# Float32 attention and two gated layers on one core: 36 subtractions of low halves go from GpSimd to VectorE

## The chip, the cores and the metric

The kernel runs on one core of one Trainium2 chip. The metric is device time in microseconds (us), the median of several executions; lower is better. Five engines work side by side, each through its own queue in order: TensorE (PE: matmuls, and PEld: weight loads), VectorE (DVE), ScalarE (ACT), GpSimd (POOL) and SyncE (SP, which here issues DMAs). An engine waits at the head of its queue for semaphores that other engines or DMAs raise.

## The reference, cut to what matters

```python
scores = scale * q @ k.T                       # 4 batches, 8 heads, 576 positions, 64 columns
scores = where(mask, scores, -1e9)             # heads 0-3: the last 32; heads 4-7: every 4th of the last 128
attn = softmax(scores) @ v                     # -> x: 2304 tokens x 512
xn = x / sqrt(mean(x * x) + 1e-6) * rms_g
g = xn @ w_gate                                # 512 -> 1536
h = (silu(g) * (xn @ w_val)) @ w_out           # 1536 -> 512
g2 = h @ w_in2                                 # 512 -> 2048
out = (maximum(g2, 0) + alpha * minimum(g2, 0)) @ w_out2
```

## The kernel before, in words

Every large product is made of float16 halves. A float32 matrix is scaled and rounded to a high half (float16), and the low half is what the rounding left out. A product then takes three matmuls: high by high, high by low and low by high. So each operand needs two element-wise steps: ScalarE writes the high half, and another engine subtracts it from the float32 value to get the low half.

**Weights.** They arrive as 64-bit floats, 128 x 512 to a block: 36 blocks for the first layer (for each c of 0 to 11 one of w_gate, w_val and w_out) and 32 for the second. `load_w` (L188) issues the DMA on SP, `decode_w` (L197) makes float32 of a block by three VectorE instructions (L202, L203, L204). A scale must be known before a block is split: for w_gate and w_val it comes from a Gram product on TensorE over a chunk of blocks (`gram_w1`, L257; c of 0 to 2 first, then 3 to 11), whose maxima go through L255, `over_partitions` (L309, a small matmul, L312) and `root_scale`. `split_w` (L377) then makes the halves. ScalarE writes the high half (L381). For two blocks of three of the first layer VectorE makes the low half in one instruction that also scales (L386). For the third, ScalarE first writes the scaled block back (L383) and GpSimd subtracts (L384). In the second layer every second block goes to GpSimd.

**Tokens.** There are seven token blocks j: 0 and 1 have 256 tokens (the first 128 positions of two batches each), 2 to 5 have 384, and 6 has 256. A stage A of a block is the first layer, a stage B the second. Stage A takes c from 0 to 11: `mm1` (L857) makes 24 matmuls into PSUM, ScalarE takes a tanh (L872), VectorE makes the product t by L873 and L874, and ScalarE writes its high half (L876). `lo` (L879) makes the low half on GpSimd (L882). `mm2` (L891) then adds both halves times w_out to the sum acc, 6 matmuls of 512 columns in blocks 0 and 1. In block 0 the `mm2` come 12 values of c late, in block 1 they follow one c behind (LAG0 and LAG).

**Attention.** Its steps (groups of queries) are interleaved with the blocks before the block that needs them. Of interest here are the normalisation of the rows (L689 on ScalarE, L690 on VectorE, a power on GpSimd, L691, and the scaled row on VectorE, L692), the transposes of those rows on TensorE (L704), and the exponentials on ScalarE (L548).

**Order.** The program is recorded in the order that `slots` and `steps` give, but the framework's scheduler then sets the order of the instructions on each engine by priority and its own estimate of times. So an edit of one function also moves others.

Of the kernel before, what the change touches and what calls it, by code (L numbers as in the profile page):

```python
# [13 lines left out]
ALU = mybir.AluOpType  # L14
# [15 lines left out]
def kernel(  # L30
# [14 lines left out]
    nc = tc.nc  # L45
# [6 lines left out]
    NW1 = 3 * C1  # L52
# [60 lines left out]
    def band(m, rows, cols, c0, lo, hi, off=0):  # L113

        view = m[0:rows, c0:c0 + cols]
        nc.gpsimd.affine_select(
            out=view, in_=view, compare_op=ALU.is_ge, fill=NEG,
            base=off - lo, pattern=[[1, cols]], channel_multiplier=-1,
        )
        nc.gpsimd.affine_select(  # L120
            out=view, in_=view, compare_op=ALU.is_ge, fill=NEG,
            base=hi - off, pattern=[[-1, cols]], channel_multiplier=1,
        )
# [43 lines left out]
    def give(*slots):  # L167
        clock_[0] += 1
        for i in slots:
            free[i] = True  # L170
            given_back[i] = clock_[0]

    def one_slot():

        i = min((i for i in range(NSLOT) if free[i]), key=lambda i: (given_back[i], i))
        free[i] = False
        return i
# [30 lines left out]
    def dec(b):  # L208
        d = dec_at[b]
        return wb[:, d * 512:(d + 1) * 512]  # L210
# [5 lines left out]
    def half(b, l):  # L216
        d = hl_at[b]
        return wb16[:, d * 1024 + l * 512:d * 1024 + (l + 1) * 512]
# [11 lines left out]
    def chunk(c):  # L230
        return max(i for i in range(NCH) if ch0[i] <= c)
# [3 lines left out]
    def scale_of(b):  # L235
        if b >= NW1:
            return S_IN + (b - NW1) % 2
        ch = chunk(b // 3)
        return 2 * NCH + ch if b % 3 == 2 else 2 * ch + b % 3
# [132 lines left out]
        nc.vector.tensor_scalar(nal, al, -1.0, None, ALU.mult)  # L372

    n_split = [0]
    LO1, LO2 = 3, 2

    def split_w(b):  # L377
        s = scale_of(b)
        n_split[0] += 1
        hl_at[b] = one_slot()  # L380
        nc.scalar.activation(half(b, 0), dec(b), ACTF.Copy, scale=wsg[:, s:s + 1])  # L381
        if n_split[0] % (LO1 if b < NW1 else LO2) == 0:
            nc.scalar.activation(dec(b), dec(b), ACTF.Copy, scale=wsg[:, s:s + 1])  # L383
            nc.gpsimd.tensor_tensor(half(b, 1), dec(b), half(b, 0), ALU.subtract)  # L384
        else:
            nc.vector.scalar_tensor_tensor(half(b, 1), dec(b), wsg[:, s:s + 1], half(b, 0), ALU.mult, ALU.subtract)  # L386
        give(dec_at.pop(b))
# [466 lines left out]
    def ncols(j):  # L854
        return blocks[j][1]

    def mm1(j, c):  # L857
        T = ncols(j)
        xt = xy[j % NXY]
        if T <= 256:  # L860
            both = psw()
            pg, pv = both[:, 0:256], both[:, 256:512]
        else:
            pg, pv = psw(), psw()
        for ps, b in ((pg, b_g(c)), (pv, b_v(c))):
            n = 0
            for kc in range(KD):
                for l, m in ((0, 0), (0, 1), (1, 0)):
                    mm(ps[:, :T], blk(b, l)[:, kc, :], xt[:, m, kc, :T], n == 0, n == 3 * KD - 1)
                    n += 1  # L870
        t = wk.tile([128, TMAX], F32, tag="w32", bufs=3, name="t")
        nc.scalar.activation(t[:, :T], pg[:, :T], ACTF.Tanh, scale=tsc[:, chunk(c):chunk(c) + 1])  # L872
        nc.vector.scalar_tensor_tensor(t[:, :T], t[:, :T], 1.0, pg[:, :T], ALU.add, ALU.mult)  # L873
        nc.vector.scalar_tensor_tensor(t[:, :T], t[:, :T], 2.0 ** -46, pv[:, :T], ALU.mult, ALU.mult)  # L874
        a = hl_take(j, c)
        nc.scalar.activation(a[:, 0, :T], t[:, :T], ACTF.Copy)  # L876
        ah[j, c] = a, t

    def lo(j, c):  # L879
        a, t = ah[j, c]  # L880
        T = ncols(j)
        nc.gpsimd.tensor_tensor(a[:, 1, :T], t[:, :T], a[:, 0, :T], ALU.subtract)  # L882

    def accumulate(j, a, b, first, last):
        for n in range(ncols(j) // 128):
# [29 lines left out]
    def mm3(j, c):  # L915
        T = ncols(j)
        yt = xy[j % NXY]
        if c == 0:
            rc = ysc[j][:, :T // 128]
            nc.vector.tensor_scalar(rc, rc, k1, None, ALU.mult)  # L920
        ps = psw()
        n = 0
        for kc in range(KD):
            for l, m in ((0, 0), (0, 1), (1, 0)):
                mm(ps[:, :T], blk(b_i(c), l)[:, kc, :], yt[:, m, kc, :T], n == 0, n == 3 * KD - 1)
                n += 1
        p = wk.tile([128, TMAX], F32, tag="w32", bufs=3, name="p")
        m = wk.tile([128, TMAX], F32, tag="w32", bufs=3, name="m")
        nc.scalar.activation(m[:, :T], ps[:, :T], ACTF.Relu, scale=-(2.0 ** -15))  # L929
        nc.scalar.activation(p[:, :T], ps[:, :T], ACTF.Relu, scale=2.0 ** -15)  # L930
        nc.vector.scalar_tensor_tensor(p[:, :T], m[:, :T], nal[:, c:c + 1], p[:, :T], ALU.mult, ALU.add)  # L931
        a = hl_take(j + 100, c)
        nc.scalar.activation(a[:, 0, :T], p[:, :T], ACTF.Copy)  # L933
        ah[j, c] = a, p
# [40 lines left out]
    def dur(s):  # L975
        return ncols(s[1]) / 128.0 * (1.95 if s[0] == "A" else 1.3)
# [12 lines left out]
    def take(d):  # L989

        rate = max([(n - state["done"]) / max(when - state["clock"], 1.0) for n, when in need] + [0.0])
        state["credit"] = min(state["credit"] + rate * d, 4.0)
        got = []
        while steps and state["credit"] >= 1.0 and len(got) < 2:
            j = steps[0][1]
            if j is not None and j >= NXY and j - NXY not in done_b:
                break
            got.append(steps.popleft()[0])
            state["done"] += 1
            state["credit"] -= 1.0  # L1000
        return got
# [15 lines left out]
    def pump(n):  # L1017

        for _ in range(n):
            if loaded:  # L1020
                b = loaded.popleft()
                decode_w(b)
                norm_w(b)
                n_done[0] += 1
                if b == b_o(C1 - 1):
                    scale_wo()
                if b == NBLK - 1:
                    scale_w2()
            fill()

    def pump_to(n):
        while n_done[0] < n:
            pump(1)
# [3 lines left out]
    def flush(kind, j, keep):  # L1037
        p = pend[kind, j]
        while len(p) > keep:
            c = p.popleft()  # L1040
            if kind == "A":
                if j == 0:
                    pump_to(NW1)
                    split_w(b_o(c))
                mm2(j, c)
                if c == C1 - 1:
                    y_out(j)
            else:
                mm4(j, c)
                if c == C2 - 1:  # L1050
                    o_out(j)
                    done_b.add(j)
# [19 lines left out]
    for b in w1[:2]:  # L1072
        split_w(b)
    for s in slots:
        kind, j, c = s
        for f in take(dur(s)):
            f()
        if (kind, j) == ("A", 0):
            pump_to(min(2 * ch0[chunk(min(c + 1, C1 - 1)) + 1], len(w1)))
            for b in w1[2 * c + 2:2 * c + 4]:  # L1080
                split_w(b)
        if kind == "A" and j < 3:
            state["spare"] = (SP0, SP1, 3)[j]
            state["pump"] = state.get("pump", 0.0) + PUMP[j]
            pump(int(state["pump"]))
            state["pump"] -= int(state["pump"])
        while (kind, j, c) == ("B", 0, 0) and (loaded or later):
            pump(1)
        if (kind, j) == ("B", 0):
            for b in range(NW1 + (2 * c + 2 if c else 0), min(NW1 + 2 * c + 4, NBLK)):  # L1090
                split_w(b)
        if kind == "A":
            mm1(j, c)
        else:
            mm3(j, c)
        lo(j, c)
        pend.setdefault((kind, j), deque()).append(c)
        state["clock"] += dur(s)
        last = c == (C1 if kind == "A" else C2) - 1
        early_one = kind == "A" and j in ahead and c < LOOK  # L1100
        flush(kind, j, 0 if last else LAG0 if (kind, j) == ("A", 0) else LOOK if early_one else LAG)
# [36 lines left out]
```

## Time and profile before

| | |
|---|---|
| median of 3 runs | 990.51 us (990.18 to 991.71) |
| the profiled execution's own time | 992.55 us |
| its span, first to last instruction | 990.8 us |
| TensorE, matmuls: busy | 927.5 us |
| VectorE: busy | 546.4 us |
| ScalarE: busy | 558.7 us |
| GpSimd: busy | 285.9 us |

The busy times are sums over stages with different limits, and a busy TensorE may still run below its peak, since its matmuls are pipelined. So the table says that TensorE fills most of the span; which engine sets the pace is to be read stage by stage.

### The profile page before, as it was taken

The numbers are of one execution on the slowest core, as the hardware profiler recorded it, in microseconds if no ns is written. First come the engines' busy times: TensorE is split into PE (matmuls) and PEld (weight loads), VectorE is DVE, ScalarE is ACT, GpSimd is POOL, SyncE is SP. The second block draws the span as 40 slices with busy tenths as digits, with TensorE's granted clock in tenths as the row PEclk, the third lists the DMA queues.
The fourth block names the chain that finished last, engine by engine and source line by source line (L and its number), as shares of the span: only waits on it lengthen the run. The fifth ranks groups of instructions, "written<-read, shape, count | busy, mean of one in ns | idle before, by whom it ended". The sixth has DMA issues, their size and how long they took to land.

```text
span 990.8 us, 17722 instructions
## 1 busy us (share of the span) xinstructions
PE 927.5 (94%) x6270; PEld 579.0 (58%) x6270; DVE 546.4 (55%) x1396; ACT 558.7 (56%) x1604; POOL 285.9 (29%) x326
## 2 busy tenths in 40 slices
PE   5468699999999999999999999999999999999997
PEld 3457576775555666655555655555555556765564
DVE  5999987899787655554535764524523122231111
ACT  3335567667798887776746776634444222243343
POOL 2121422121244555333333233223233121122222
PEclk9777899999999999999999999999999999999999
DMA  9992426446543544433535443222210001010000
GB/s 249 315 360 66 130 78 167 127 140 194 105 89 55 103 76 95 98 83 76 122 63 82 96 97 76 50 75 56 42 25 15 33 6 21 13 22 1 1 32 22
DMA packets 191607, 88.06 MB, mean 89 GB/s; under 512 B 176800, under 2 KB 180384, under 8 KB 191520
## 3 DMA queue, kind: packets, MB, share of 16 engines
q1 hardware_dynamic: 188896, 82.22, 34.2%
q10 hardware_dynamic: 2624, 4.72, 1.4%
q8 instruction: 49, 0.80, 0.3%
q14 instruction: 38, 0.31, 0.1%
HBM read 55.32 MB, written 6.55 MB: 62 GB/s over the span
## 4 chain that ended last, share of the span: by engine, by line
PE 69%; DVE 13%; DMA 7%; ACT 4%; issue 4%; SPq 2%; POOL 1%; DVEq 0%; ACTq 0%; POOLq 0%
PE psw L92 40%; PE acc L92 28%; DVE wb L203 3%; DVE wb L204 2%; DMA wb<-in_q_dram 2%; DVE wb L202 2%; DVE wb L386 1%; DMA rkv<-in_v_dram 1%; ACT s L548 1%; DMA wb<-in_moe_w_gate_dram 1%; DVE t L874 1%; SPq L584 1%; ACT wb L381 1%; DMA wb<-in_moe_w_out_dram 1%; DVE t L873 1%
## 5 line engine op out<-in xcount | busy, mean ns | idle before, releaser
L92 PEld LDWEIGHTS <-wb 128*128 128x128 f16 (+1 forms) x4014 | 388.6, 99 | 237.6 <-issue 7.6
L92 PE MATMUL psw<-xy,wb 128*128 128x384 f16 (+1 forms) x3360 | 525.4, 305 | 1.5 <-DVE t L874 1.1
L92 PE MATMUL acc<-wb,hl 128*128 128x512 f16 x1002 | 246.9, 381 | 4.9 <-ACT hl L876 2.0
L931 DVE SCALAR_TENSOR_TENSOR p<-m,nal,p 128x384 f32<-128x384 f32 (+1 forms) x112 | 68.1, 608 | 161.8 <-ACT p L930 160.8
L92 PEld LDWEIGHTS <-hl 128*128 128x128 f16 x1002 | 96.0, 98 | 98.3 <-POOL hl L882 3.5
L92 PE MATMUL acc<-wb 128*128 128x512 f16 x510 | 123.3, 379 | 0.4 <-ACT wb L933 0.4
L882 POOL TENSOR_TENSOR hl<-t,hl 128x384 f16<-128x384 f32 (+1 forms) x56 | 51.9, 927 | 173.4 <-ACT hl L876 152.7
L882 POOL TENSOR_TENSOR hl<-p,hl 128x384 f16<-128x384 f32 (+1 forms) x74 | 61.4, 829 | 122.5 <-ACT hl L933 111.6
L872 ACT ACTIVATE t<-psw,tsc 128x384 f32<-128x384 f32 (+1 forms) x84 | 44.2, 527 | 83.8 <-PE psw L92 77.4
L929 ACT ACTIVATE m<-psw 128x384 f32<-128x384 f32 (+1 forms) x112 | 48.6, 434 | 66.3 <-PE psw L92 64.8
L873 DVE SCALAR_TENSOR_TENSOR t<-t,psw 128x384 f32<-128x384 f32 (+1 forms) x84 | 41.1, 489 | 77.9 <-ACT t L872 77.8
L92 PE MATMUL psw<-wb 128*128 128x128 bf16 (+6 forms) x448 | 55.0, 294 | 9.3 <-DVE wb L204 6.6
L658 POOL TENSOR_TENSOR phl<-s,phl 96x512 f16<-96x512 f32 (+2 forms) x33 | 36.9, 1117 | 75.2 <-ACT phl L652 45.1
L548 ACT ACTIVATE s<-s,mx 96x128 f32<-96x128 f32 (+2 forms) x132 | 50.1, 381 | 13.1 <-DVE mx L545 12.8
L381 ACT ACTIVATE wb<-wb,wsg 128x512 f16<-128x512 f32 x68 | 46.1, 711 | 19.2 <-DVE wsg L319 14.1
L874 DVE SCALAR_TENSOR_TENSOR t<-t,psw 128x384 f32<-128x384 f32 (+1 forms) x84 | 41.2, 490 | 27.6 <-PE psw L92 26.5
L882 POOL TENSOR_TENSOR wb<-t,wb 128x256 f16<-128x256 f32 (+1 forms) x28 | 23.7, 847 | 109.9 <-ACT wb L876 101.7
L384 POOL TENSOR_TENSOR wb<-wb 128x512 f16<-128x512 f32 x28 | 37.4, 1337 | 46.5 <-ACT wb L383 36.7
L933 ACT ACTIVATE hl<-p 128x384 f16<-128x384 f32 (+1 forms) x74 | 34.5, 466 | 27.7 <-DVE p L931 27.6
L882 POOL TENSOR_TENSOR wb<-p,wb 128x384 f16<-128x384 f32 (+1 forms) x38 | 32.3, 849 | 61.7 <-ACT wb L933 51.8
L930 ACT ACTIVATE p<-psw 128x384 f32<-128x384 f32 (+1 forms) x112 | 48.7, 435 | 0.0
L204 DVE SCALAR_TENSOR_TENSOR wb<-wb 128x512 int32<-128x512 int32 x68 | 48.6, 718 | 0.1
(159 smaller groups left out, 1077.2 us busy)
## 6 DMA issues: line engine op xcount, KB each, us to landing
wb<-in_moe_w_out_dram SPq DMA_DIRECT2D x28, 512.0 KB, 4.3
wb<-in_moe_w_in_dram SPq DMA_DIRECT2D x16, 512.0 KB, 3.7
wb<-in_moe_w_gate_dram SPq DMA_DIRECT2D x12, 512.0 KB, 7.3
wb<-in_moe_w_val_dram SPq DMA_DIRECT2D x12, 512.0 KB, 6.8
out_dram<-o ACTq DMA_DIRECT2D x16, 256.0 KB, 2.3
rkv<-in_k_dram SPq DMA_DIRECT2D x23, 128.0 KB, 2.7
rkv<-in_v_dram SPq DMA_DIRECT2D x23, 128.0 KB, 2.8
rq<-in_q_dram SPq DMA_DIRECT2D x23, 96.0 KB, 2.1
```

Of the source, the lines that this page charges most:

```text
L92: nc.tensor.matmul(o, a, b, start=start, stop=stop)
L204: nc.vector.scalar_tensor_tensor(w, r[:, :, 0], 29, w, ALU.logical_shift_right, ALU.bitwise_or)
L381: nc.scalar.activation(half(b, 0), dec(b), ACTF.Copy, scale=wsg[:, s:s + 1])
L384: nc.gpsimd.tensor_tensor(half(b, 1), dec(b), half(b, 0), ALU.subtract)
L548: nc.scalar.activation(s[:nq, h, :nk], s[:nq, h, :nk], ACTF.Exp, bias=mx[:nq, 1, h:h + 1], accum_out=g["dn"][:nq, h])
L872: nc.scalar.activation(t[:, :T], pg[:, :T], ACTF.Tanh, scale=tsc[:, chunk(c):chunk(c) + 1])
L873: nc.vector.scalar_tensor_tensor(t[:, :T], t[:, :T], 1.0, pg[:, :T], ALU.add, ALU.mult)
L874: nc.vector.scalar_tensor_tensor(t[:, :T], t[:, :T], 2.0 ** -46, pv[:, :T], ALU.mult, ALU.mult)
L882: nc.gpsimd.tensor_tensor(a[:, 1, :T], t[:, :T], a[:, 0, :T], ALU.subtract)
L929: nc.scalar.activation(m[:, :T], ps[:, :T], ACTF.Relu, scale=-(2.0 ** -15))
L930: nc.scalar.activation(p[:, :T], ps[:, :T], ACTF.Relu, scale=2.0 ** -15)
L931: nc.vector.scalar_tensor_tensor(p[:, :T], m[:, :T], nal[:, c:c + 1], p[:, :T], ALU.mult, ALU.add)
```

## The change

Two things move from GpSimd to VectorE. In `split_w`, no block of the first layer goes the GpSimd way any more: 12 of its 36 blocks lose the second ScalarE pass (L383) and the GpSimd subtraction (L384) and get one VectorE instruction (L386) instead. In `lo`, the low half of the product t of blocks 0 and 1 in stage A is subtracted on VectorE: 24 instructions of 128 x 256. The other blocks, stage B and the second layer's weights stay as they were. TensorE has the same instructions.

```diff
     n_split = [0]
-    LO1, LO2 = 3, 2
+    LO2 = 2
 
     def split_w(b):
         s = scale_of(b)
         n_split[0] += 1
         hl_at[b] = one_slot()
         nc.scalar.activation(half(b, 0), dec(b), ACTF.Copy, scale=wsg[:, s:s + 1])
-        if n_split[0] % (LO1 if b < NW1 else LO2) == 0:
+        if b >= NW1 and n_split[0] % LO2 == 0:
             nc.scalar.activation(dec(b), dec(b), ACTF.Copy, scale=wsg[:, s:s + 1])
             nc.gpsimd.tensor_tensor(half(b, 1), dec(b), half(b, 0), ALU.subtract)
         else:
...
-    def lo(j, c):
+    def lo(j, c, quiet):
         a, t = ah[j, c]
         T = ncols(j)
-        nc.gpsimd.tensor_tensor(a[:, 1, :T], t[:, :T], a[:, 0, :T], ALU.subtract)
+        (nc.vector if quiet else nc.gpsimd).tensor_tensor(
+            a[:, 1, :T], t[:, :T], a[:, 0, :T], ALU.subtract)
...
-        lo(j, c)
+        lo(j, c, kind == "A" and j < 2)
```

The scheduler's order differs from the first split on, on every engine. The last difference lies, on VectorE, at instruction 544 of 1,396 of the kernel before, one of the first softmax steps beside stage A of block 2; behind that every engine has the same instructions in the same order as before. (The names of tiles: wb is the pool of weight slots, wsg a scale, xy the tokens that stage A multiplies, t the product, hl its halves, psw and psw in PSUM the matmul results.)

The first place is VectorE at the splits of the first chunk. Before:

```order
L692 SCALAR_TENSOR_TENSOR wb<-wb,ms,gs 128x512
L204 SCALAR_TENSOR_TENSOR wb<-wb 128x512
L386 SCALAR_TENSOR_TENSOR wb<-wb,wsg 128x512 x2
L204 SCALAR_TENSOR_TENSOR wb<-wb 128x512
L386 SCALAR_TENSOR_TENSOR wb<-wb,wsg 128x512 x2
L202 TENSOR_SCALAR wb<-wb 128x512 x3
L706 TENSOR_TENSOR xy_73<-psw,xy_73 128x4x128
```

Now:

```order
L692 SCALAR_TENSOR_TENSOR wb<-wb,ms,gs 128x512
L204 SCALAR_TENSOR_TENSOR wb<-wb 128x512
L386 SCALAR_TENSOR_TENSOR wb<-wb,wsg 128x512 x2
L204 SCALAR_TENSOR_TENSOR wb<-wb 128x512
L386 SCALAR_TENSOR_TENSOR wb<-wb,wsg 128x512 x3
L202 TENSOR_SCALAR wb<-wb 128x512
L386 SCALAR_TENSOR_TENSOR wb<-wb,wsg 128x512
L202 TENSOR_SCALAR wb<-wb 128x512
L706 TENSOR_TENSOR xy_73<-psw,xy_73 128x4x128
```

Six low halves stand there instead of four, ahead of the block's last tokens (L706).

The second place is ScalarE at the last two splits of the second chunk of w_gate and w_val. Before:

```order
L599 ACTIVATE wb<-psw 128x2x96
L600 ACTIVATE wb<-psw 128x256
L381 ACTIVATE wb<-wb,wsg 128x512 x2
L383 ACTIVATE wb<-wb,wsg 128x512
L872 ACTIVATE t<-psw,tsc 128x256
L876 ACTIVATE wb<-t 128x256
```

Now:

```order
L599 ACTIVATE wb<-psw 128x2x96
L600 ACTIVATE wb<-psw 128x256
L381 ACTIVATE wb<-wb,wsg 128x512 x2
L872 ACTIVATE t<-psw,tsc 128x256
L876 ACTIVATE wb<-t 128x256
```

The tanh (L872) follows the high halves at once.

The third place is VectorE ahead of the last normalised rows that block 1 brings (L692, the fourth with 96 rows), in the second half of stage A of block 1. Before:

```order
L690 TENSOR_SCALAR ms<-ms 96x1
L204 SCALAR_TENSOR_TENSOR wb<-wb 128x512
L556 RECIPROCAL dn<-dn 96x4
L204 SCALAR_TENSOR_TENSOR wb<-wb 128x512
L202 TENSOR_SCALAR wb<-wb 128x512
L204 SCALAR_TENSOR_TENSOR wb<-wb 128x512
L692 SCALAR_TENSOR_TENSOR wb<-wb,ms,gs 96x512
```

Now:

```order
L690 TENSOR_SCALAR ms<-ms 96x1
L202 TENSOR_SCALAR wb<-wb 128x512
L882 TENSOR_TENSOR hl_108<-t,hl_108 128x256
L204 SCALAR_TENSOR_TENSOR wb<-wb 128x512
L873 SCALAR_TENSOR_TENSOR t<-t,psw 128x256
L204 SCALAR_TENSOR_TENSOR wb<-wb 128x512
L203 SCALAR_TENSOR_TENSOR wb<-wb 128x512
L692 SCALAR_TENSOR_TENSOR wb<-wb,ms,gs 96x512
```

A low half (L882) now stands in that queue, and waits there for its high half from ScalarE.

## Rows read from the trace of the kernel before

**Rows 1.** The page: TensorE and VectorE busy in 40 equal slices of the span, in tenths.

```profile
PE   5468699999999999999999999999999999999997
...
DVE  5999987899787655554535764524523122231111
```

**Rows 2.** Stretches: length; busy us (count) of PE, PEld, DVE, ACT, POOL; granted clock; DMA.

```profile
50.90:126.90 76.00, 54.00 (x449) 46.97 (x448) 73.19 (x154) 37.98 (x94) 20.80 (x18) 0.82 0.53 180
126.90:160.00 33.10, 32.69 (x227) 21.87 (x227) 27.61 (x65) 23.17 (x67) 9.58 (x9) 0.95 0.34 97
...
187.00:225.00 38.00, 36.86 (x300) 28.29 (x301) 36.64 (x90) 25.36 (x88) 8.92 (x10) 1.00 0.45 133
```

**Rows 3.** Waits of TensorE, 50.9 to 126.9 us: total us, times, longest.

```profile
PE psw L704 <- DVE wb L692: 17.5, 3, 10.0
PE psw L92 <- DVE wb L204: 6.6, 1, 6.6
```

**Rows 4.** Timeline of VectorE from 50.9 us: start, us, line, operation, out<-in, count.

```profile
50.90 1.41 DVE L386 SCALAR_TENSOR_TENSOR wb<-wb,wsg 128x512 f16<-128x512 f32 x2
52.22 0.69 DVE L204 SCALAR_TENSOR_TENSOR wb<-wb 128x512 int32<-128x512 int32 x1
52.83 3.22 DVE L386 SCALAR_TENSOR_TENSOR wb<-wb,wsg 128x512 f16<-128x512 f32 x2
```

**Rows 5.** Timeline of GpSimd at the same time; in brackets its idle time before, and the releaser.

```profile
51.83 3.66 POOL L384 TENSOR_TENSOR wb<-wb 128x512 f16<-128x512 f32 x2 [2.23 <-ACT wb L383]
```

**Rows 6.** VectorE by line, 50.9 to 126.9 us: count, busy us, mean ns, idle before.

```profile
L204 DVE SCALAR_TENSOR_TENSOR wb<-wb 128x512 int32<-128x512 int32 x23 | 16.6, 726 | 0.0
L203 DVE SCALAR_TENSOR_TENSOR wb<-wb 128x512 int32<-128x512 int32 x21 | 15.6, 759 | 0.0
L386 DVE SCALAR_TENSOR_TENSOR wb<-wb,wsg 128x512 f16<-128x512 f32 x16 | 14.8, 938 | 0.8 <-ACT wb L381 0.8
L202 DVE TENSOR_SCALAR wb<-wb 128x512 int32<-128x512 int32 x21 | 9.7, 476 | 0.0
...
L555 DVE TENSOR_SCALAR dn<-dn 128x4 f32<-128x4 f32 x4 | 1.1, 284 | 0.0
```

**Rows 7.** VectorE by line, 19 to 47 us.

```profile
L203 DVE SCALAR_TENSOR_TENSOR wb<-wb 128x512 int32<-128x512 int32 x10 | 6.8, 679 | 0.0
L204 DVE SCALAR_TENSOR_TENSOR wb<-wb 128x512 int32<-128x512 int32 x9 | 6.1, 682 | 0.0
L202 DVE TENSOR_SCALAR wb<-wb 128x512 int32<-128x512 int32 x11 | 4.6, 416 | 0.0
...
L555 DVE TENSOR_SCALAR dn<-dn 128x4 f32<-128x4 f32 x4 | 0.6, 161 | 0.2 <-ACT wb L548 0.2
```

**Rows 8.** All instructions of line 386: shortest, median and longest ns.

```profile
L386 DVE SCALAR_TENSOR_TENSOR wb<-wb,wsg x40: 728/745/1647, 50.9 to 313.9; 128x512 f16<-128x512 f32 x40
```

**Rows 9.** GpSimd by line, 50.9 to 126.9 us.

```profile
L384 POOL TENSOR_TENSOR wb<-wb 128x512 f16<-128x512 f32 x8 | 12.6, 1582 | 29.0 <-ACT wb L383 25.6 <-issue 3.5
L882 POOL TENSOR_TENSOR wb<-t,wb 128x256 f16<-128x256 f32 x8 | 7.2, 894 | 24.3 <-ACT wb L876 24.3
```

**Rows 10.** Timeline of ScalarE behind the last splits of the second chunk.

```profile
124.66 0.72 ACT L383 ACTIVATE wb<-wb,wsg 128x512 f32<-128x512 f32 x1
```

**Rows 11.** Timeline of VectorE right behind that.

```profile
125.78 0.42 DVE L873 SCALAR_TENSOR_TENSOR t<-t,psw 128x256 f32<-128x256 f32 x1 [0.97 <-ACT t L872]
```

**Rows 12.** Timeline of TensorE at the last transposes that block 1 brings.

```profile
224.70 0.52 PE L704 MATMUL psw<-ident,wb 96*128 96x96 f32 x4 [1.14 <-DVE wb L692]
```

**Rows 13.** VectorE by line, 187.4 to 223.8 us.

```profile
L203 DVE SCALAR_TENSOR_TENSOR wb<-wb 128x512 int32<-128x512 int32 x12 | 8.7, 730 | 0.0
L204 DVE SCALAR_TENSOR_TENSOR wb<-wb 128x512 int32<-128x512 int32 x12 | 8.4, 710 | 0.0
```

**Rows 14.** Timelines of VectorE and ScalarE: one product t of block 1, and its high half.

```profile
191.21 0.41 DVE L874 SCALAR_TENSOR_TENSOR t<-t,psw 128x256 f32<-128x256 f32 x1
...
192.49 0.41 ACT L876 ACTIVATE hl<-t 128x256 f16<-128x256 f32 x1
```

## The prediction

> **What bounds the kernel now.** I read the page's slices first, then busy times by stretch, then TensorE's waits, and last the costs by line. In the slices TensorE (PE) is full from the seventh on, so from some 150 us to the end; only the first sixth of the span has holes, and there VectorE (DVE) shows 9s [rows 1]. The table by stretch makes this exact: from 50.9 us (the first split) to 126.9 us (the last Gram maximum of the first layer) VectorE is busy 73.19 of 76.00 us and TensorE 54.00; from 126.9 to 160 us it is the other way round, 27.61 of VectorE against 32.69 of 33.10 for TensorE [rows 2]. TensorE's waits name the same: in the first stretch it waits 17.5 us for normalised rows (L692) and 6.6 us for decoded weights (L204), both VectorE's [rows 3]. So a microsecond on VectorE counts in full up to 126.9 us. Later it counts only where TensorE is caught waiting for it, which in 187 to 225 us happens with 1.14 us at one place (L704 behind L692) [rows 12], although VectorE is busy 36.64 of 38.00 us there [rows 2].
>
> The views by line show what the moved work did to VectorE from the other engine. Two L386 took 1.32 us from start to start of the next instruction while GpSimd stood still, 0.66 us each; the next two, beside two L384, took 3.22 us together [rows 4, 5]. So the two engines hinder each other, and the sum has a term on either side.
>
> **The change part by part.** Durations are of the profiled execution, which took 992.55 us, 2.04 us above the median of the runs, 990.51 us; I add the difference to the median.
>
> *First stretch, to 126.9 us, added.* Of the 12 splits that change, 8 lie here, of the 24 low halves of t 8 ran on GpSimd here [rows 9] and 9 stand in VectorE's new queue up to the same point. A split costs 0.66 us [rows 4]: 8 x 0.66 = 5.3 us. Records overlap by 0.08 us (median 0.745 against 0.66) [rows 4, 8]. A subtraction of 128 x 256 with both inputs in SBUF is in no row. Its nearest row is L873, 128 x 256 with one input in PSUM, 0.42 us [rows 11], so 0.34 us in the queue; the upper bound is the 0.66 us of an L386, which has twice the columns. I take 0.34, since size and number of inputs agree: 9 x 0.34 = 3.1 us. Added: 8.4 us.
>
> *First stretch, removed.* GpSimd no longer stretches VectorE's instructions. Against the stretch without GpSimd [rows 7], and for L386 against its median, the means [rows 6] fall by 726 - 682 = 44 ns for 23 L204 (1.0 us), 759 - 679 = 80 ns for 21 L203 (1.7), 938 - 745 = 193 ns for 16 L386 [rows 8] (3.1), 476 - 416 = 60 ns for 21 L202 (1.3) and 284 - 161 = 123 ns for 4 L555 (0.5). Together 7.6 us. That is nearly all that was added: 8.4 - 7.6 = +0.8 us.
>
> *ScalarE.* Twelve L383 go. Eight lie in this stretch, but ScalarE is busy only 37.98 of 76 us [rows 2], so seven are worth nothing: the cover is VectorE, and without it each would be worth its 0.64 us (0.72 less the overlap) [rows 10]. The last one counts: L872 stands behind L383, and VectorE's L873 sits idle 0.97 us for L872 [rows 10, 11]. In the new order L872 follows the high halves at once. -0.6 us. Subtotal at 126.9 us: +0.2 us. TensorE's order up to there is the old one but for a few swapped neighbours, so it arrives with the same work done.
>
> *126.9 to 187 us.* Four splits and seven low halves more on VectorE; TensorE is full, VectorE has 5.5 us free up to 160 us alone [rows 2], and the low halves of block 0 are used some twelve values of c later. Nothing. If that cover were gone, it would cost 4 x 0.66 + 7 x 0.34 = 5.0 us.
>
> *187 to 225 us.* Here VectorE has 1.4 us free [rows 2], and TensorE is caught at L704. In front of the L692 that L704 waits for the new queue has, counted from 187.4 us, 6 low halves and one L203 more and one L874 less: 6 x 0.34 + 0.60 - 0.34 = 2.3 us. Gone is the stretch of 12 L203 (51 ns) and 12 L204 (28 ns), 0.9 us, and some 0.3 us on small ones [rows 13, 7]. Net 1.1 us later, and the wait of 1.14 us grows to some 2.2 us, since TensorE has the same matmuls in front of it: +1.1 us.
>
> *Behind that.* TensorE is full, and from about 256 us every queue is the old one. No term. SP's queue keeps its loads, a few in another order.
>
> **Sum:** 0.2 + 1.1 = +1.3 us: 993.9 us for the profiled execution, **991.8 us** for the median. 0.2% is 2.0 us, about what a measurement here can tell from no change, so I forecast "the same".
>
> **A rule against the trace.** By the 16 GpSimd instructions of the first stretch [rows 9] VectorE lost 7.6 us, about 0.5 us each. The two L384 of the first pair took 3.66 us, and VectorE lost 3.22 - 1.32 = 1.9 us beside them, half of that [rows 4, 5]. The Trainium skill, page "SBUF — State Buffer", section "Who interferes with whom", states that a VectorE instruction with two SBUF inputs and a GpSimd instruction that reads SBUF exclude each other, and that whichever comes second stands still until the first is done. The trace agrees that these two hinder each other, but shows no standstill for the whole length on average; with one for every pair the sum would be that of the first rival.
>
> **Rivals.**
>
> *Faster, every GpSimd instruction stops VectorE for its whole length.* As a mechanism of this kernel: the 8 L384 and 8 L882 are busy 12.6 + 7.2 = 19.8 us [rows 9]; if all of it had stopped VectorE, 19.8 us go instead of 7.6, and the result is 991.8 - 12.2 = 979.6 us. For it: both L386 beside the first pair were caught [rows 4]. Against: VectorE was busy 73.19 of 76.00 us with the lengths that I took [rows 2, 6], which leaves no hidden 12 us. 5%.
>
> *Faster, TensorE keeps its clock.* In 126.9 to 160 us TensorE is full, yet its granted clock is 0.95, so 3.3 us ran at 1.2 instead of 2.4 GHz, which cost 1.65 us [rows 2]. That fall stands behind the waits for L692 [rows 3]. If VectorE delivers those rows earlier (its stretch goes before its new work comes), the fall is away, and if L882 comes out of the way of the L692 of block 1 as well, L704's waits of 1.1 + 1.1 us go too: 991.8 - 1.65 - 2.2 = 988.0 us. Against: my count has the third L692 at no gain. 17%.
>
> *Slower, low halves hold VectorE's queue.* L882 needs L876's high half, on another engine. That came 1.28 us behind t's product at one place (191.62 to 192.90) [rows 14], since exponentials stood in front of it. GpSimd could wait; VectorE's in-order queue cannot, and decoding, products and rows for the next block stand behind. The new order leaves under 1.3 us of other work between product and L882 at 3 of the 12 values of c of block 1. With some 0.7 us lost at each, 2.1 us, and no slack in 187 to 225 us, TensorE pays all: 991.8 + 2.1 = 993.9 us. If L882 costs its upper bound as well, 15 x 0.32 = 4.8 us more, 998.7 us. It decides from 0.7 us on, that is from one full wait. For it: VectorE's 1.4 free us [rows 2]. Against: some of these waits only replace waits of the neighbours for the same engine. 33%.
>
> **How the numbers follow.** The forecast has 45%, all within 0.2%. Slower: the third rival, 33%. Faster: 5% + 17% = 22%. The range runs from 987.0 us, just past the second rival, to 997.0 us, which takes in the third rival and two thirds of L882's upper bound; left out are the first rival and the far ends, some 15%.
>
> **What would show it.** In the new profile: L386 near its 0.745 us and L202 to L204 near their quiet means throughout 50 to 160 us; L882 on VectorE at about 0.42 us; VectorE still full from 51 us to about 127 us, and the last Gram maximum there at 127 us, give or take 1; TensorE's wait for L692 near 225 us at some 2 us; then the same idle times as before. Wrong would be: a last maximum before 124 us (the first or second rival), waits of L882 for L876 on VectorE of over 2 us together with TensorE waiting for L882 (the third), or a fall of the clock that is gone.

## The result, and the profile after

The changed kernel took 995.70 us (median of 4 runs, 994.78 to 996.72), the kernel before, run beside it, 991.11 us (990.18 to 991.97). The two medians are 4.6 us apart; the ratio that goes with the runs is 1.0052, with a 95% interval of 1.0039 to 1.0064, which is 5.2 us. So the change made the kernel slower by some 5 us. That lies inside the range of 987.0 to 997.0 us, but not where the forecast stood (991.8 us, no change). It is the side of the third rival. (All ratios below are of this kind; they differ from the quotient of the two medians by up to 0.7 promille.) The profiled execution of the changed kernel took 996.72 us, with a span of 994.9 us.

The busy times by stretch come first (columns as in [rows 2]); the last row is a piece of the two above it.

```profile
50.90:126.90 76.00, 54.10 (x446) 46.66 (x444) 73.62 (x170) 32.99 (x85) 2.72 (x2) 0.80 0.51 177
126.90:160.00 33.10, 32.98 (x225) 21.48 (x226) 27.78 (x74) 21.07 (x66) 0.00 (x0) 0.95 0.41 119
187.00:225.00 38.00, 34.85 (x283) 26.35 (x280) 36.53 (x93) 25.41 (x89) 7.62 (x4) 0.99 0.44 137
225.00:257.00 32.00, 30.69 (x183) 19.00 (x184) 26.82 (x70) 21.03 (x61) 4.57 (x3) 0.90 0.58 153
224.30:231.10 6.80, 5.79 (x31) 4.75 (x32) 5.12 (x12) 4.30 (x14) 0.08 (x1) 0.50 0.69 239
```

Up to 160 us it is the old picture [rows 2]: VectorE full, TensorE about as busy, the granted clock 0.95 again in 126.9 to 160 us. Only GpSimd is nearly empty now (2.72 and 0.00 us). The difference begins at 187 us: TensorE is busy 34.85 us there instead of 36.86, and from 224.3 us on, the end of a wait of TensorE, lie 6.8 us at a granted clock of 0.50, that is at 1.2 instead of 2.4 GHz. The same 6.8 us of the kernel before:

```profile
224.30:231.10 6.80, 6.40 (x52) 4.89 (x53) 6.80 (x16) 4.93 (x17) 0.67 (x1) 1.00 0.81 295
```

There TensorE did 52 matmuls in that time, now 31. The timeline of TensorE, changed kernel, shows what stands ahead of the fall (start, us, line, operation, out<-in, count; in brackets the idle time before and its releaser):

```profile
218.93 2.32 PE L92 MATMUL acc<-wb,hl 128*128 128x512 f16 x10
221.89 0.60 PE L92 MATMUL acc<-wb,hl 128*128 128x512 f16 x2 [0.65 <-DVE hl L882]
225.31 0.88 PE L704 MATMUL psw<-ident,wb 96*128 96x96 f32 x4 [2.81 <-DVE wb L692]
225.97 0.42 PE L92 MATMUL psw<-xy,wb 128*128 128x256 f16 x1
226.19 1.43 PE L92 MATMUL psw<-wb 128*96 128x64 f32 x8
```

And VectorE's timeline at the same place:

```profile
218.96 0.41 DVE L882 TENSOR_TENSOR hl<-t,hl 128x256 f16<-128x256 f32 x1
219.29 0.68 DVE L203 SCALAR_TENSOR_TENSOR wb<-wb 128x512 int32<-128x512 int32 x1
...
221.42 0.41 DVE L882 TENSOR_TENSOR hl<-t,hl 128x256 f16<-128x256 f32 x1
221.76 0.68 DVE L204 SCALAR_TENSOR_TENSOR wb<-wb 128x512 int32<-128x512 int32 x1
...
224.41 0.75 DVE L692 SCALAR_TENSOR_TENSOR wb<-wb,ms,gs 96x512 f32<-96x512 f32 x1 [0.44 <-POOL ms L691]
```

TensorE first waits 0.65 us for a low half that stands behind decoding, then 2.81 us at L704 for the normalised rows; before, the wait at this place was 1.14 us [rows 12].

To see where time goes without trusting single instructions, whose order differs, I counted TensorE's work: the columns of all its 6,270 matmuls that had started by a given time (float32 ones counted twice), divided by 2,400 to a figure in us. (With the mean time of each form of matmul at full clock as the weight instead, no entry below moves by more than 0.4 us.) The table shows how far each kernel's profiled execution is behind the kernel before (minus: ahead). The experiments are explained below; 0.66 us of any difference may come from the start, since the first split of the changed kernel already lies that much earlier (50.98 against 51.64 us, its end). The execution of the kernel before that the table measures against took 992.55 us, 1.4 us above the median of 991.11 us, so a line can end lower than the medians say.

| behind before, us, at | 127 | 160 | 214 | 235 | 257 | 309 | 450 us | median of the runs against before |
|---|---|---|---|---|---|---|---|---|
| the change | 0.0 | -1.7 | -1.9 | +3.5 | +4.5 | +4.7 | +4.3 | 1.0052 |
| splits alone | +0.1 | -1.5 | -2.9 | +2.7 | +2.6 | +1.9 | +0.5 | 1.0009 |
| low halves alone | -0.7 | -0.4 | +0.2 | +4.3 | +4.3 | +3.2 | +1.8 | 1.0037 |
| without block 1 | 0.0 | -1.7 | -1.9 | +3.8 | +3.7 | +3.0 | +2.4 | 1.0006 |
| without block 0 | -0.8 | -3.5 | -4.3 | -1.6 | +5.3 | +3.8 | +3.2 | 1.0052 |
| less decoding, the change | 0.0 | -2.3 | -2.9 | -3.5 | -2.2 | -0.1 | +5.3 | 1.0079 |
| early decoding (blocks 0 to 2), the change | +2.1 | +1.2 | -0.2 | -1.3 | +3.5 | +3.3 | -2.2 | 0.9976 |

Read the first line: nothing gained or lost up to 127 us, a lead of 1.9 us by 214 us, and 5.4 us lost between 214 and 235 us, at the end of block 1. Of these the two waits make 0.65 + 2.81 - 1.14 = 2.3 us, and 5.79 busy us at half the clock instead of full make 2.9 us; together 5.2 us. That is the account of one profiled execution; the experiments show that the medians do not follow this stall alone.

The first stretch in the views by line. VectorE, 50.9 to 126.9 us (columns as in [rows 6]):

```profile
L386 DVE SCALAR_TENSOR_TENSOR wb<-wb,wsg 128x512 f16<-128x512 f32 x24 | 17.4, 741 | 0.8 <-ACT wb L381 0.8
L204 DVE SCALAR_TENSOR_TENSOR wb<-wb 128x512 int32<-128x512 int32 x22 | 14.7, 681 | 0.0
L203 DVE SCALAR_TENSOR_TENSOR wb<-wb 128x512 int32<-128x512 int32 x21 | 14.1, 681 | 0.0
L202 DVE TENSOR_SCALAR wb<-wb 128x512 int32<-128x512 int32 x21 | 8.5, 416 | 0.0
L882 DVE TENSOR_TENSOR wb<-t,wb 128x256 f16<-128x256 f32 x9 | 3.7, 416 | 0.2 <-ACT wb L876 0.2
```

Against [rows 6] the means fell from 938 to 741, 726 to 681, 759 to 681 and 476 to 416 ns: the quiet means of [rows 7] and the median of [rows 8], to some ns. The low half costs 416 ns, or 0.34 us in the queue (218.96 to 219.29 above). The waits of TensorE in that stretch changed names more than their sum (compare [rows 3]):

```profile
PE psw L92 <- DVE wb L204: 8.5, 1, 8.5
PE psw L704 <- DVE ms L690: 5.2, 1, 5.2
PE psw L92 <- DVE diag L309: 4.4, 1, 4.4
PE psw L704 <- DVE wb L692: 1.8, 1, 1.8
```

And VectorE's timeline behind the last Gram maximum of the first layer, where L309 began at 126.89 us before:

```profile
126.34 0.43 DVE L882 TENSOR_TENSOR wb<-t,wb 128x256 f16<-128x256 f32 x1 [0.19 <-ACT wb L876]
126.68 0.28 DVE L309 TENSOR_SCALAR diag<-ident,sqo 128x128 bf16<-128x128 f32 x1
```

The subtraction ahead of it is the new one, and its 0.19 us is the only wait of any low half for its high half that the waits of VectorE list for the changed kernel between 50.9 and 260 us.

### The profile page after: what moved, and what is told of

It is laid out like the page before. It is cut to its first block, busy times and chain, and to the rows that moved or that the text cites. A ratio compares the mean times of both kernels' runs of the same rounds, so it can differ in the third digit from the quotient of the medians.

```text
span 994.9 us, 17674 instructions
## 1 busy us (share of the span) xinstructions
PE 928.5 (93%) x6270; PEld 580.1 (58%) x6270; DVE 547.9 (55%) x1432; ACT 551.7 (55%) x1592; POOL 253.7 (26%) x290
## 4 chain that ended last, share of the span: by engine, by line
PE 67%; DVE 12%; DMA 8%; ACT 5%; issue 3%; SPq 3%; POOL 1%; ACTq 0%; POOLq 0%; DVEq 0%
PE psw L92 39%; PE acc L92 27%; DVE wb L204 2%; DVE wb L203 2%; DMA rkv<-in_v_dram 1%; DMA wb<-in_moe_w_out_dram 1%; DVE wb L386 1%; ACT s L548 1%; DVE wb L202 1%; SPq L195 1%; DMA wb<-in_moe_w_val_dram 1%; DMA rkv<-in_k_dram 1%; ACT junk L481 1%; DVE t L873 1%; DMA wb<-in_moe_w_gate_dram 1%
## 5 line engine op out<-in xcount | busy, mean ns | idle before, releaser
L882 POOL TENSOR_TENSOR hl<-p,hl 128x384 f16<-128x384 f32 (+1 forms) x74 | 61.4, 830 | 122.3 <-ACT hl L934 110.0
L872 ACT ACTIVATE t<-psw,tsc 128x384 f32<-128x384 f32 (+1 forms) x84 | 44.3, 528 | 78.5 <-PE psw L92 77.5
L691 POOL TENSOR_TENSOR ms<-ms,mhalf 96x1 f32<-96x1 f32 (+2 forms) x24 | 21.9, 913 | 225.6 <-DVE ms L690 206.2
L882 POOL TENSOR_TENSOR hl<-t,hl 128x384 f16<-128x384 f32 (+1 forms) x44 | 42.4, 963 | 137.9 <-ACT hl L876 137.9
L874 DVE SCALAR_TENSOR_TENSOR t<-t,psw 128x384 f32<-128x384 f32 (+1 forms) x84 | 41.2, 490 | 27.8 <-PE psw L92 26.6
L882 POOL TENSOR_TENSOR wb<-p,wb 128x384 f16<-128x384 f32 (+1 forms) x38 | 32.4, 852 | 62.9 <-ACT wb L934 52.7
L204 DVE SCALAR_TENSOR_TENSOR wb<-wb 128x512 int32<-128x512 int32 x68 | 46.4, 690 | 0.1
L203 DVE SCALAR_TENSOR_TENSOR wb<-wb 128x512 int32<-128x512 int32 x68 | 45.5, 681 | 0.1
```

What stands on the lines that cost most here:

```text
L203: nc.vector.scalar_tensor_tensor(w, r[:, :, 1], -0x40000000, w, ALU.bitwise_and, ALU.bitwise_or)
L204: nc.vector.scalar_tensor_tensor(w, r[:, :, 0], 29, w, ALU.logical_shift_right, ALU.bitwise_or)
L882: (nc.vector if quiet else nc.gpsimd).tensor_tensor(a[:, 1, :T], t[:, :T], a[:, 0, :T], ALU.subtract)
```

## The experiments

The theory behind the first four: the low halves of block 1 make VectorE late at the end of block 1, TensorE stalls at L704, and its clock falls.

**Only the splits.**

```diff
-        lo(j, c, kind == "A" and j < 2)
+        lo(j, c, False)
```

> Only the 12 splits go to VectorE; all low halves of t are on GpSimd as before. Theory (the low halves of block 1 make VectorE late between 187 and 225 us, TensorE then stalls at L704 near 225 us and its clock falls behind that): within 1.5 us of before (991.1 us), no window at 1.2 GHz between 215 and 260 us, L704's wait there about 1.1 us as before. Rival A (the 12 splits are what costs, since a microsecond of VectorE counts in full up to 127 us): 994 to 996 us, with the last Gram maximum of the first layer over 2 us later than in before. Rival B (neither half of the change costs by itself, only both together): within 1 us of before.

Measured: 992.53 us (12 runs, 989.61 to 995.18), ratio 1.0009 [0.9996, 1.0022]. The time is that of the theory, and rival A is out: TensorE is 0.1 us behind at 127 us, so 12 splits on VectorE cost nothing there. But two of the signs that I named did not come. TensorE does stall near 220 us, though at another instruction, and the clock does fall behind it (granted clock 0.84 in 214 to 235 us). TensorE's timeline of this kernel:

```profile
220.99 1.04 PE L92 MATMUL acc<-wb,hl 128*128 128x512 f16 x4 [1.61 <-ACT hl L876]
224.12 1.04 PE L92 MATMUL acc<-wb,hl 128*128 128x512 f16 x2 [2.09 <-POOL hl L882]
224.95 0.85 PE L704 MATMUL psw<-ident,wb 96*128 96x96 f32 x4
```

The high half is late because of VectorE's product L874, which stands behind decoding and ends only at 220.49 us. So this stall is not the work of block 1's low halves alone. This kernel was 2.9 us ahead at 214 us, and from 257 to 450 us it gets 2.1 us back. Part of the lead is the clock: in 126.9 to 160 us it is granted 1.00 here, against 0.95 before and with the whole change.

**Only the low halves.**

```diff
-    LO2 = 2
+    LO1, LO2 = 3, 2
...
-        if b >= NW1 and n_split[0] % LO2 == 0:
+        if n_split[0] % (LO1 if b < NW1 else LO2) == 0:
```

> Only the 24 low halves of blocks 0 and 1 go to VectorE; 12 splits go through ScalarE and GpSimd as before. Theory: 994 to 997 us, with L704 waiting some 2 to 3 us near 225 us and a window at 1.2 GHz behind it. Rival A (splits): within 1 us of before, 991 us. Rival B (only both together): within 1.5 us of before and no new window at 1.2 GHz.

Measured: 994.50 us (8 runs, 993.23 to 999.96), ratio 1.0037 [1.0020, 1.0055], with the clock at 1.2 GHz for 3.4 us behind the stall. L704 waited 1.3 us, less than expected, and a high half (L876) held TensorE for 3.4 us. By the medians the loss goes with the low halves.

**Without block 1.**

```diff
-        lo(j, c, kind == "A" and j < 2)
+        lo(j, c, kind == "A" and j < 1)
```

> The change without block 1: 12 splits and the 12 low halves of block 0 on VectorE, the 12 low halves of block 1 back on GpSimd. Theory: the whole loss goes, 990 to 992 us, L704 near 225 us waits about 1 us, no window at 1.2 GHz between 215 and 260 us. Rival A (splits): stays at 994 to 996 us. Rival C (each moved instruction costs its share, wherever it stands): about 994 us, the loss less a third.

Measured: 992.45 us (11 runs, 990.95 to 995.23), ratio 1.0006 [0.9997, 1.0015]. The loss is gone, and rivals A and C are out. Again the sign at 220 us is a miss: in the profiled execution the stall and the fall of the clock are there, as with the splits alone. That execution was the slowest of the eleven (995.23 us), so its line in the table shows more loss than the median has. Still, the stall with its 6.8 us at half the clock stands in two kernels whose medians lose nothing, so it is not by itself what the change costs.

**Without block 0.**

```diff
-        lo(j, c, kind == "A" and j < 2)
+        lo(j, c, kind == "A" and j == 1)
```

> The change without block 0: 12 splits and the 12 low halves of block 1 on VectorE, the 12 low halves of block 0 on GpSimd. Theory: the loss stays, 994 to 997 us, with TensorE waiting for L882 or L692 between 215 and 226 us and a window at 1.2 GHz behind. Rival A (splits): the same time, but lost before 127 us. Rival C (each moved instruction costs its share): about 994 us.

Measured: 996.47 us (6 runs, 995.50 to 998.14), ratio 1.0052 [1.0037, 1.0066]: all of the loss. But it came by another way than expected. TensorE waits near 220 us, and yet its clock stays at 1.00 in 214 to 235 us, and at 235 us it is still ahead of before. It loses 6.9 us between 235 and 257 us, behind the last low half of block 1 (VectorE makes it at 232.82 us), in the first steps of block 2. The longest wait there is for a DMA of the attention, and the clock falls behind it (254.3 to 257.7 us). TensorE's timeline:

```profile
218.84 0.60 PE L92 MATMUL acc<-wb,hl 128*128 128x512 f16 x2 [0.30 <-DVE hl L882]
221.66 0.52 PE L704 MATMUL psw<-ident,wb 96*128 96x96 f32 x4 [2.21 <-DVE wb L692]
...
252.98 0.42 PE L92 MATMUL psw<-qkT 128*96 128x128 f16 x4 [3.19 <-DMA qkT<-qkhl]
```

VectorE is not full in that stretch: it is busy 14.51 of 22.00 us and stands 7.0 us at L202 for loads of weight blocks. How the low halves of block 1 bring this about, no run takes apart.

So by the ratios of the runs the loss sits with the 12 low halves of block 1, whatever the wait that passes it on: 1.0052 - 1.0006 is 4.5 us (the change against the run without block 1), and 1.0052 - 1.0009 is 4.3 us (the run without block 0 against the splits alone). The intervals allow some 1.5 to 2 us either way, and the medians alone give 3.5 and 3.9 us. Their whole time in VectorE's queue is 12 x 0.34 = 4.1 us.

**A dummy in their place.** Is it VectorE's time, or the wait for ScalarE at the head of its queue? Low halves of block 1 on GpSimd again, and behind each L874 of block 1 a subtraction of the same size that waits for no other engine:

```diff
+        if j == 1:
+            d = wk.tile([128, DM], F32, tag="st", bufs=2, name="o")
+            nc.vector.tensor_tensor(d.bitcast(F16)[:, :T], t[:, :T], t[:, :T], ALU.subtract)
         a = hl_take(j, c)
...
-        lo(j, c, kind == "A" and j < 2)
+        lo(j, c, kind == "A" and j < 1)
```

> Block 1's low halves back on GpSimd (as in the run without block 1, 992.5 us), but one VectorE subtraction of the same size (128 x 256, result unused) behind each of block 1's 12 products, with no high half of ScalarE to wait for. Theory: VectorE's 12 x 0.34 = 4.1 us are what costs, 995 to 997 us. Rival D: the waiting is what costs, so 992 to 993.5 us.

Measured: 998.12 us (6 runs, 997.49 to 998.83), ratio 1.0074 [1.0060, 1.0088]: 5.7 us over the run without block 1 (6.7 by the ratios), and more than the change itself. So no waiting is needed for the loss; rival D is out. That it is more than the dummies' own 5.5 us is not explained; the dummies also give the queues a new order. The dummies by line, 150 to 240 us, and TensorE's waits of that kernel, 214 to 260 us (its L877, L879 and L885 are the dummy, L876 and L882):

```profile
L877 DVE TENSOR_TENSOR o<-t 128x256 f16<-128x256 f32 x12 | 5.5, 456 | 0.0
```

```profile
PE psw L92 <- DVE t L874: 2.7, 1, 2.7
PE acc L92 <- ACT hl L879: 2.3, 1, 2.3
PE acc L92 <- DVE yhl L914: 1.6, 1, 1.6
PE psw L704 <- DVE wb L692: 0.6, 1, 0.6
```

All of these but the second name VectorE, and the high half of the second had itself waited 1.66 us for a product (L874). Eleven of the dummies took 405 to 426 ns and one 891, so they are the size of the low halves they stand for. Here too most is lost behind 235 us: TensorE is 1.4 us behind before there and 7.8 us at 257 us.

**Less decoding in block 1.** If VectorE's load is the cause, taking other load away must cure it. PUMP is the number of the second layer's weight blocks decoded per value of c in blocks 0, 1 and 2.

```diff
-    PUMP = (1.5, 1.5, 2.0)
+    PUMP = (1.5, 1.0, 2.5)
```

> The whole change, but in block 1 one block of the second layer's weights is decoded per value of c instead of 1.5 (the rest in block 2): by the last normalised rows of block 1 VectorE has 16 decoding instructions less in front. Theory (the loss comes from VectorE being full between 187 and 226 us, so that any instruction there is late for TensorE): the stall at c = 21 to 22 and L704 goes, no window at 1.2 GHz between 215 and 235 us, and the time falls from 995.7 to 991 us or below. Rival D (low halves wait for ScalarE's high half at the head of VectorE's queue, whatever else is in it): 994 to 996 us, TensorE still waits for L882 or L692 there.

Measured: 998.57 us (6 runs, 997.04 to 1000.18), ratio 1.0079 [1.0063, 1.0095]. The place is cured and the time is worse. At 235 us TensorE is 3.5 us ahead of before, where the change was 3.5 us behind; L704 waits 0.5 us, and the granted clock is 1.00 in 214 to 235 us and on to 400 us. The loss now comes behind 309 us: TensorE in 309 to 400 us, first this kernel, then before.

```profile
309.00:400.00 91.00, 80.03 (x606) 52.69 (x604) 61.61 (x138) 79.18 (x232) 49.01 (x55) 1.00 0.41 82
```

```profile
309.00:400.00 91.00, 85.54 (x655) 57.40 (x653) 52.62 (x138) 72.02 (x224) 44.42 (x52) 0.98 0.45 86
```

VectorE has 9.0 us more to do there. Nine low halves of the second layer's weights (L386) stand in that stretch, 8.4 us of VectorE, against two before: the work that was put off falls due in the first stage B, and TensorE is not covered there either.

**The same with 1.25 blocks.**

```diff
-    PUMP = (1.5, 1.5, 2.0)
+    PUMP = (1.5, 1.25, 2.25)
```

> The whole change with 1.25 blocks decoded per value of c in block 1 instead of 1.5 (9 decoding instructions less in front of block 1's last normalised rows). Theory: less load there and less work left for stage B than with 1: 991 to 994 us. Rival E: 995 us or more.

Measured: 994.23 us (5 runs, 993.53 to 994.88), ratio 1.0034 [1.0021, 1.0048]: just above the expected range. TensorE is 2.1 us ahead at 235 us and 2.7 us behind at 450 us, the same exchange at half the size.

**Less decoding, splits alone, and before.** Both with PUMP = (1.5, 1.0, 2.5), on the kernel with the splits alone and on the kernel before.

> Splits alone on VectorE, low halves on GpSimd, and one block decoded per value of c in block 1 instead of 1.5. The splits alone had TensorE some 3 us ahead of before at 206 to 214 us and lost it by waits of 3.7 us behind VectorE at 219 to 224 us. Theory: with VectorE freer there the waits go and the 3 us stay: 988 to 990 us. Rival D, and a rival by which the lead is only work put off: 991 to 993 us.

> The kernel before with one block decoded per value of c in block 1 instead of 1.5, as the measure for the other two. Theory: L704's wait of 1.1 us near 225 us goes, 989.5 to 991.5 us; a gain of the two others beyond this one is then the change's own.

Measured: 994.07 us (7 runs, 993.40 to 995.06), ratio 1.0032 [1.0018, 1.0045], and 991.18 us (12 runs, 990.02 to 991.80), ratio 0.9999 [0.9987, 1.0010]. The first is a miss. Its waits near 220 us shrink from 3.7 to 1.5 us and the clock stays at 1.00 there, but at 214 us it led by 1.2 us instead of 2.9, and at 450 us it is 2.7 us behind. On before the time is as expected, but not the sign: L704 still waits 0.9 us. TensorE is 2.7 us ahead at 235 us and even at 450 us, so here too the work only moves, at no cost.

**Decoding moved forward.** VectorE is free 6.1 of the 27 us from 160 to 187 us of the changed kernel. Here more is decoded early:

```diff
-            state["pump"] = state.get("pump", 0.0) + PUMP[j]
+            state["pump"] = state.get("pump", 0.0) + (2.5 if c < 4 else 1.0 if j == 1 else PUMP[j])
```

This edit does more than the expectation below says. Python reads it as 2.5 for the first four values of c of all three blocks, 0, 1 and 2; only the 1.0 behind them is for block 1 alone. So decoding moves forward from block 0 on: 38 blocks are decoded by 126.9 us instead of 36, 52 by 187 us instead of 46, and the last of the 68 begins at 251.0 instead of 259.8 us (L202, counted).

> The whole change, with block 1's decoding of the second layer's weights moved forward: 2.5 blocks per value of c for c below 4, 1 from there on, instead of 1.5 throughout, so the total by the end of block 1 is kept (the run with one per c throughout was 4.6 us ahead of before at 232 us, and lost 8 us behind 309 us). VectorE has 6.1 us free in 160 to 187 us of the changed kernel. Theory (the stall comes from VectorE's load between 187 and 226 us, the later loss of the earlier run from weights that came late for stage B): 991 to 993.5 us. Rival E (the scheduler's new order, whatever it is, costs some us around 220 us): 995 us or more.

Measured: 988.01 us (11 runs, 986.81 to 990.20), ratio 0.9976 [0.9966, 0.9987]: 2.9 us faster than before beside it (990.90 us; 2.4 us by the ratio), better than expected and faster than either kernel. The stretches 160 to 187 and 187 to 225 us, and TensorE's timeline at L704:

```profile
160.00:187.00 27.00, 26.94 (x220) 18.73 (x219) 26.12 (x76) 19.53 (x76) 0.00 (x0) 1.00 0.86 224
187.00:225.00 38.00, 38.00 (x323) 29.59 (x322) 34.59 (x92) 27.08 (x95) 2.90 (x4) 1.00 0.48 138
```

```profile
222.01 1.46 PE L92 MATMUL acc<-wb,hl 128*128 128x512 f16 x6
223.39 0.52 PE L704 MATMUL psw<-ident,wb 96*128 96x96 f32 x4
```

VectorE now fills the earlier stretch (26.12 us instead of 20.88), has 3.4 us free in the later one, TensorE is busy 38.00 of 38.00 us, and L704 waits for nothing. At 235 us TensorE is 4.8 us earlier than in the change. The rest is less simple. At 127 us it is 2.1 us behind, where the change was level (with the same edit before is 2.3 us behind there, the splits alone 0.3); from 235 to 257 us it loses 4.8 us, and from 309 to 450 us it gains 5.5 us. What the move in block 1 alone would give, no run shows.

**The same on the splits alone and on before.** The edit is again that of blocks 0 to 2.

> Splits alone on VectorE, low halves on GpSimd, decoding moved forward in block 1 as in the other run. Theory: the lead of 3 us at 214 us is kept, 988 to 990.5 us. Rival E: 992 to 994 us as before this edit.

> The kernel before with decoding moved forward in block 1, as the measure for the other two. Theory: L704's wait of 1.1 us goes and little else, 989.5 to 991.5 us. Rival E: anything up to 994 us.

Measured: 995.02 us (5 runs, 993.50 to 997.34), ratio 1.0048 [1.0034, 1.0061], and 993.60 us (9 runs, 991.70 to 996.71), ratio 1.0024 [1.0012, 1.0036]. The first is a clear miss, by 4.5 us; the second falls to rival E. Both cure the end of block 1 (TensorE 2.7 and 1.1 us ahead at 235 us) and lose it by 257 us, the splits alone with a wait of 3.8 us for a scale of the attention (L498). So in these three runs the earlier decoding pays only together with the low halves on VectorE: 988.0 against 993.6 and 995.0 us. Why it does, I can't say. The edit gives every engine a new order far into the second layer's first stages, and no run takes that apart.

## Why the prediction was right or wrong

The forecast was +1.3 us and the change cost 4.6. The measured time lies in the stated range because the range was stretched for the third rival, whose mechanism did not happen; that much is luck.

**What bounds the kernel: right.** VectorE stayed full to 127 us and TensorE behind it.

**First stretch: right, in sum and in its terms.** Forecast +0.2 us at 126.9 us; measured, TensorE's work 0.0 us behind and the step behind the last Gram maximum (L309) 0.2 us earlier (126.68 against 126.89 us), or 0.45 us later when the 0.66 us at the start are taken off. The low half cost the 0.34 us of its nearest row. The quiet means came back as forecast, L555 too (162 ns). So a loss of VectorE to GpSimd of 0.5 us per GpSimd instruction, against a cost of 0.34 or 0.66 us per instruction moved, is a wash.

**126.9 to 187 us, "nothing": wrong, in the change's favour.** TensorE was 1.7 us ahead at 160 us, and 2.1 to 2.6 us ahead at 175 to 187 us with the splits alone. No wait of TensorE in 126.9 to 187 us explains it (0.8 us in all before, 1.2 us after). With the splits alone the clock accounts for some of it (1.00 instead of 0.95 up to 160 us, worth the 1.65 us of the second rival); in the change, with the clock as before, what did is open.

**187 to 225 us, "+1.1 us": the step that failed.** It saw the right place and the right wait and stopped there. L692 came 0.6 us later (I had 1.1), but the wait grew to 2.81 us, not 2.2, and 0.65 us for L882 stood ahead of it, because TensorE came earlier with the lead I had not counted: 1.14 + 0.6 + 1.9 = 3.6 us, against 0.65 + 2.81 = 3.5. The larger part of what this execution lost was not in the sum at all: behind the stall 6.8 us ran at a granted clock of 0.50, another 2.9 us. I had a fall of the clock as something that could go (the second rival), not as something that a longer wait brings. The profiled executions with the splits alone, the low halves alone and without block 1 show such a fall behind their stalls too; the one without block 0 stalls for 0.30 + 2.21 us and shows none there.

**"Behind that: no term": wrong by its reason.** I priced the low halves in front of one L692, six of the twelve, and took 0.9 us off for the stretch that is gone. The runs charge all twelve with about their full queue time, 3.5 to 4.5 us against 12 x 0.34 = 4.1 us. The loss goes on behind 225 us, also where VectorE isn't full: without block 0 TensorE lost 6.9 us from 235 to 257 us. So a full TensorE and old queues from 256 us on were no reason for "no term": in that run the loss was paid in the first steps of block 2, by waits that my sum did not look at.

**The rivals.** The first (whole-length block, 979.6 us) is out: with 19.8 us gone instead of 7.6 the first stretch would have shrunk by some 12 us, and it kept its length. The Trainium skill, page "SBUF — State Buffer", section "Who interferes with whom", calls the contention an exclusive lock; the trace shows less on average, 0.5 us lost beside a GpSimd instruction of 1.2 us. The second (988.0 us) did not happen: the clock in 126.9 to 160 us is 0.95 as before. I had also read its row wrongly: the fall of the kernel before begins at 129.4 us, behind a wait of 0.83 us for L309, while the last wait for L692 in that stretch ended at 118.92 us. And the clock is 1.00 there in profiled executions where the last of these L692 begins no earlier than before (118.04 us): with the splits alone at 118.36, with early decoding on before at 119.92 us. So its fall there does not hang on L692 alone. The third was right in side and size (993.9 us, 998.7 us at its end), and wrong in its mechanism: low halves waited 0.19 us in all for ScalarE, and dummies that wait for nothing cost 5.7 us. The point from which it decides was the one it named, that VectorE has no slack there; what decides is instructions, not waits.

**The chances.** Slower had 33%, no change 45%. The argument for "no slack" was in the text and spoke for slower; it should have carried over from the wait at L704 to every instruction added between 187 and 240 us.

**What stays open.** The table and the medians agree on the sign of each edit to the change, but profiled executions lie up to 3 us from their medians, and a new order alone can move the time: the kernel before with its decoding moved forward is slower by 2.4 promille at the same work. Every edit above gives the queues a new order too, and none holds the order still, so a part of each difference may be order. That the 12 low halves of block 1 on VectorE go with the loss is shown by five kernels (the change, the splits, the low halves, without block 1, without block 0). By which wait TensorE pays it is not: the stall at 220 us stands in kernels without the loss, and the loss in a kernel that takes it behind 235 us. How it divides between the stall, the clock and the steps up to 257 us is not settled to better than some 2 us.

## What to carry to other kernels

Before work is moved to an engine, take its free time stretch by stretch, and charge everything that lands in a full stretch in full, not only what stands ahead of the one wait that the trace shows today. If the move saves contention elsewhere, look for other work of that engine that can go from the full stretch into a freer one: here decoding earlier in three blocks went with 2.9 us gained instead of 4.6 us lost, though on two near kernels the same edit lost. Follow what comes late into the next stage, also where the engine has time again. A wait that the bounding engine takes can cost more than its length, because the clock behind it can fall, as it did in some of these runs; read the granted clock of the stretch behind every new wait.

## What the runs showed of the hardware that I had not expected

- A stall of TensorE of some 3.5 us (0.65 + 2.81) amid full work was followed by 6.8 us at a granted clock of 0.50; with splits alone the stall was 3.7 us, with the clock at 0.84 in 214 to 235 us. In the runs without the stall (less or early decoding on the change) the clock was 1.00 there.
- The length of a wait did not tell whether the clock would fall. In the kernel before, a wait of 2.05 us (310.6 to 312.66 us) was followed by 3.4 us at 0.51. With less decoding on before, a wait of 3.48 us (up to 324.65 us) was not: the clock is 1.00 in all of 309 to 400 us.
- A new order of the same instructions can cost more than half of what the change does: the kernel before with its decoding moved forward in blocks 0 to 2 took 993.60 us against 990.90 us, with TensorE busy 38.00 of 38.00 us in 187 to 225 us.
